# Attention issued from one written list of tasks, with a buffer for each pair's transposed V

## The chip, the cores and the metric

One Trainium2 chip, one core of it. The metric is device time in microseconds (us) of one execution; the median of several executions is compared. Five queues matter: PE (TensorE), DVE (VectorE), ACT (ScalarE), POOL (GpSimd) and SP (SyncE, which issues nearly all DMAs here). Each runs its instructions strictly in the order in which they stand in its program, and waits on semaphores of the others.

## What is computed

Sparse attention over 2 batches of 8 heads (768 positions of 64), then two MLP blocks. All in float32.

```python
def _attn_ref(q, k, v):                       # S = 768, block 32, window 16
    k_sum = k.reshape(B, H, nb, block, D).max(axis=3)
    v_sum = v.reshape(B, H, nb, block, D).mean(axis=3)
    scores_l = scale * q @ k.T                # kept where |i - j| < window
    scores_s = scale * q @ k_sum.T + log(block)
    a = softmax(concat([scores_l masked, scores_s]))
    return a @ concat([v, v_sum])
...
x = attn_out as (B, S, 512)
h = relu(x.T @ w_tok1) @ w_tok2;  u = x + h.T      # tokens, 256 wide
x = u + relu(u @ w_ch1) @ w_ch2                    # channels, 1536 wide
xn = (x - mean) / sqrt(var + 1e-6) * g_ln
out = x + relu(xn @ w2_ch1) @ w2_ch2               # channels, 2048 wide
```

## The kernel before

**Pairs and quads.** Two heads share the 128 partitions and make a *pair*; there are 8 pairs (0 to 3 are batch 0). A pair's 768 rows go in 12 windows of 64 rows, four of them a *quad*: quad n = 3i + qd belongs to pair i, n runs from 0 to 23. A window has 96 keys around it and 24 block keys, 120 columns (`NK`).

**One quad, step by step** (methods of `Kern`): `att_qk` puts the scores into one of two score banks (PE). `att_exp` does two things, for each of four windows: a DVE instruction adds the mask and takes the row's extreme (L453), an ACT instruction takes the exponential (L463). `att_tr` transposes the weights on PE (L470), `att_evac` copies them to SBUF on ACT (L477), `att_av` multiplies by V (PE, L489), `att_norm` divides and stores into `u` (DVE, L503, L506).

**One pair.** `load_pair` issues K and Q on SP; `prep_k` takes the block maximum of K on DVE (L338), `copy_k` writes it into the K tile on ACT (L348). For pairs 0 to 3 V comes transposed into `VT` (`load_vt`, L318): `prep_v1` sums blocks of 32 (for pair 0 one DVE reduce, L360; for pairs 1 to 3 a tree of ten POOL additions, L366 to L370), `prep_v2` writes the sums into `VT` (ACT, L386), `att_vtr` transposes four windows on PE (L409) and `att_vev` copies them into `V` (ACT L418 for the first quad of a pair, DVE L420 for the others). For pairs 4 to 7 V is loaded in its final form (`load_v`) and only its sums are made, from `vt`: a POOL tree (L377, L380), one transpose on PE (L395), ACT (L397), POOL copies (L401). K, Q and V have three buffers, `VT` two.

**Work of the next block inside attention.** `g1(b, hf)` is x.T @ w_tok1 in pieces of twelve PE passes (L518), `g2(b)` the second token product in pieces of six matmuls (L300 to L302), `transpose_u` the transposes of u (L561). `fill` issues matmuls on zeros whose result nobody reads (L1125). Beside it the first weights are loaded (`load_half`, tiles `stage`, three buffers) and converted: `words` on ACT (L131), `decode` on DVE (L149, L154), `split_hi` on ACT (L201), `split_lo` on DVE (L226). Halves 0 to 2 hold the token weights (`tok`).

**What sets the order.** `attention` gives each of these steps a number, quad index plus an offset from the table `ORDER`, sorts, and calls them in that order. Only PE is under `manual_schedule`: its instructions stand as called. DVE, ACT, POOL and SP are ordered by the framework's scheduler from its own estimates and from priorities. The first loads and twelve fills are called in `run`, ahead of `attention`.

```python
ORDER = {
    "load_k": -5.2, "load_vt": -5.1, "load_v": -4.7, "kmax": -1.3, "copy_k": -1.0, "vsum": -2.4,
    "vput": -0.2, "vsum0": 0.55, "vput0": 1.6, "exp": 0.5, "tr": 1.1, "evac": 1.55, "av": 2.15,
    "norm": 2.6, "vtr": 1.3, "vev": 1.4, "load_vk": -2.65, "lo": 2.7, "conv": 3.5, "bg": 8.58, "fin": 0.97,
}
```

After attention come the channel MLPs, here the *main part*; its first instruction on PE is the matmul of the tile g_('u', 0)_3.

Of the kernel before, what the change touches and what calls it, by code (L numbers as in the profile page):

```python
# [20 lines left out]
P = 128  # L21
# [30 lines left out]
NT = 4  # L52
SCALE = 1.0 / math.sqrt(D)
# [6 lines left out]
class Kern:  # L60
# [46 lines left out]
    def conv_tick(self):  # L107

        nc = self.nc
        n = self.tick  # L110
        self.tick += 1
        lag = self.lag
        if 0 <= n - lag + 1 < NHALF:
            self.split_hi(n - lag + 1)
        if self.wide:
            if n < NHALF:
                yield from self.words(n)
            if 0 <= n - 1 < NHALF:
# [22 lines left out]
    def decode(self, h):  # L141


        nc = self.nc
        t = self.raw.pop(h)
        m = self.dec[h].bitcast(U32)
        put = nc.vector.scalar_tensor_tensor
        if h < EARLY or h % 2:
            nc.vector.tensor_scalar(m, m, 3, None, op0=ALU.logical_shift_left)  # L149
            yield  # L150
            if h < EARLY:
                yield
                yield
            put(m, t[:, :, 0], 29, m, op0=ALU.logical_shift_right, op1=ALU.bitwise_or)  # L154
        else:
            put(m, t[:, :, 1], 3, m, op0=ALU.logical_shift_left, op1=ALU.bitwise_or)  # L156

    def conversion(self):

        while self.tick < NHALF + self.lag:  # L160
            h = self.tick - self.lag + 1
            if 1 <= h <= NHALF and h - 1 not in self.half:
# [19 lines left out]
    def load_half(self, h):  # L182
        if self.wide:
# [7 lines left out]
    def split_hi(self, h):  # L191
        x = self.dec[h] if self.wide else self.raw[h]
        if h < 3:
            if not self.wide:
                self.nc.scalar.copy(self.tok[:, h], x)
            return
# [116 lines left out]
    def flat_vt(self, i):  # L313
        return self.VT[i % 2].rearrange("p v c -> p (v c)")

    def load_vt(self, i):
        if i < NT:
            self.nc.sync.dma_start(self.VT[i % 2][:, 0:6, NB : NB + 160], self.vk[i])  # L318
        else:
            self.nc.sync.dma_start(self.flat_vt(i)[:, 0:S], self.vt[i - NT])  # L320
# [12 lines left out]
    def prep_k(self, i):  # L333
# [3 lines left out]
        with self.tc.issue_after(self.ttr[3 * i - 2].ins) if i > 0 else ExitStack():  # L337
            nc.vector.tensor_reduce(  # L338
                ks.rearrange("p (v j) -> p v j", v=6),
                K[:, 0:6, NB + 16 : NB + 144].rearrange("p v (j k) -> p v j k", k=BLOCK),  # L340
                axis=AX.X,
                op=ALU.max,
            )
        self.ks[i] = ks

# [6 lines left out]
    def prep_v1(self, i):  # L352
        nc = self.nc
        if i < NT:
            zs = self.att.tile([P, NB], F32, tag="vs", bufs=2, name=f"vs{i}")
            x = self.VT[i % 2][:, 0:6, NB + 16 : NB + 144].rearrange("p v (j k) -> p v j k", k=BLOCK)
            z = zs.rearrange("p (v j) -> p v j", v=6)
            if i == 0:
                with self.tc.issue_after(self.ttr[0].ins):
                    nc.vector.tensor_reduce(z, x, axis=AX.X, op=ALU.add)  # L360
            else:
                for v in (0, 3):
                    half = self.att.tile([P, NB // 2, BLOCK // 2], F32, tag="vh", bufs=1, name=f"vh{i}_{v}")
                    h = half.rearrange("p (v j) k -> p v j k", v=3)
                    n = BLOCK // 2
                    nc.gpsimd.tensor_tensor(h, x[:, v : v + 3, :, 0:n], x[:, v : v + 3, :, n : 2 * n], op=ALU.add)  # L366
                    while n > 2:
                        n //= 2
                        nc.gpsimd.tensor_tensor(half[:, :, 0:n], half[:, :, 0:n], half[:, :, n : 2 * n], op=ALU.add)
                    nc.gpsimd.tensor_tensor(zs[:, 4 * v : 4 * v + 12], half[:, :, 0], half[:, :, 1], op=ALU.add)  # L370
# [3 lines left out]
        cur = self.flat_vt(i)[:, 0:S].rearrange("p (n k) -> p n k", k=BLOCK)  # L374
# [7 lines left out]
    def prep_v2(self, i):  # L382
        nc = self.nc
        if i < NT:
            zs = self.vs.pop(i)
            nc.scalar.activation(  # L386
                self.VT[i % 2][:, :, 0:NB],
# [5 lines left out]
        V, Z = self.V[i % 3].rearrange("p (j w) c -> p j w c", j=2), self.Z[i % 2]  # L393
        ps = self.ps_pt.tile([P, 512], F32, tag="pt", name=f"psv{i}")
        nc.tensor.transpose(ps[:NK, 0:P], Z, self.ident)  # L395
        src = self.att.tile([NK, P], F32, tag="zs", bufs=1, name=f"zs{i}")
        nc.scalar.activation(src, ps[:NK, 0:P], AF.Copy, scale=1.0 / BLOCK)  # L397
# [14 lines left out]
    def att_vev(self, n):  # L412
        nc = self.nc
# [28 lines left out]
    def att_exp(self, n):  # L442
# [5 lines left out]
        pr = self.att.tile([P, 4, NK], F32, tag="pr", bufs=3, name=f"pr{n}")  # L448
        self.pr[n] = pr
        for u in range(4):  # L450
            w = 4 * qd + u
            mv = w % 2 if 0 < w < NW - 1 else 2 + w % 2
            self.ttr[n] = nc.vector.tensor_tensor_reduce(  # L453
# [9 lines left out]
            nc.scalar.activation(pr[:, u], sn[:, u], AF.Exp, bias=mn[:, u : u + 1], scale=-1.0)  # L463
# [49 lines left out]
    def g1(self, b, hf):  # L513
        nc = self.nc
        for t in range(2):
            ps = self.ps_mm.tile([P, 512], F32, tag="mm", name=f"g1_{b}_{hf}_{t}")
            for st in range(ST):
                nc.tensor.matmul(  # L518
                    ps[:, :256],
                    self.tok1(st, t),  # L520
                    self.u[:, b * ST + st, 256 * hf : 256 * hf + 256],
                    start=st == 0,
                    stop=st == ST - 1,
                )
            yield
            cs = slice(256 * hf, 256 * hf + 256)
            hh, hl = self.hh[b][:, t, cs], self.hl[b][:, t, cs]
            nc.scalar.activation(hh, ps[:, :256], AF.Relu)
            nc.vector.scalar_tensor_tensor(hl, ps[:, :256], 0.0, f32(hh), op0=ALU.max, op1=ALU.subtract)  # L529
            yield  # L530

    def g2(self, b):
        nc = self.nc
        for st in range(ST):
# [20 lines left out]
    def transpose_u(self, g):  # L555
        nc = self.nc
        th, tl = self.new_xt(("u", g))
        for cc in range(CC):
# [6 lines left out]
            nc.scalar.copy(th[:, cc], ps[:, :GN])  # L565
            nc.vector.tensor_tensor(tl[:, cc], ps[:, :GN], f32(th[:, cc]), op=ALU.subtract)
# [501 lines left out]
    def attention(self):  # L1068


        npair, nq = B * NPAIR, 3 * B * NPAIR
        O = ORDER
        ev = []
        put = lambda at, *fns: ev.append((at, len(ev), fns))
        for i in range(npair):
            at = 3 * i
            if i > 1:
                put(at + O["load_k"], lambda i=i: self.load_pair(i))
                put(at + O["load_vt" if i > NT + 1 else "load_vk"], lambda i=i: self.load_vt(i))
                put(at + O["load_v"], lambda i=i: self.load_v(i))  # L1080
            put(at + (O["kmax"] if i != 1 else -0.46), lambda i=i: self.prep_k(i))
            put(at + (O["copy_k"] if i != 1 else -0.44), lambda i=i: self.copy_k(i))
            put(at + O["vsum"] if i else O["vsum0"], lambda i=i: self.prep_v1(i))
            put(at + O["vput"] if i else O["vsum0"] + 0.01, lambda i=i: self.prep_v2(i))
        for n in range(nq):
            put(n, lambda n=n: self.att_qk(n))
            if n < O["bg"]:
                put(n + 0.02, lambda: self.fill(2))
                put(n + 0.25, lambda n=n: self.fill(1 if 2 < n + 1 < 3 * NT else 2))
            if n < 3 * NT:  # L1090
                put(n + O["vtr"], lambda n=n: self.att_vtr(n))
                put(n + O["vev"], lambda n=n: self.att_vev(n))
            put(n + O["exp"], lambda n=n: self.att_exp(n))
            put(n + O["tr"], lambda n=n: self.att_tr(n))
            put(n + O["evac"], lambda n=n: self.att_evac(n))
            put(n + O["av"], lambda n=n: self.att_av(n))
            put(n + O["norm"], lambda n=n: self.weave(self.att_norm(n), self.convert(self.ops)))
        put(0.0, lambda: self.load_half(0), lambda: self.load_half(1))
        put(O["conv"], lambda: setattr(self, "ops", 4))
        put(O["bg"], lambda: setattr(self, "ops", 2))  # L1100
# [319 lines left out]
```

## Time and profile before

| | |
|---|---|
| median of 3 executions | 594.06 us (592.63 to 597.55) |
| the profiled execution | 593.27 us, span of its trace 591.5 us, mean granted clock 0.986 |
| busy over the span | PE 567.7 us (96%), DVE 405.8, ACT 271.8, POOL 30.0 |
| moved by DMA | 135.76 MB |
| first score matmul | 6.38 us after the span's start |
| end of the score matmuls of quad 11 | 56.14 us |
| first matmul of the main part | 114.20 us |

Times of day in the trace count from the span's start. A busy time of PE is not PE at its peak: neighbouring matmuls overlap in the records, so the price of a piece is taken from its start to the next one's start. "Granted clock" is 1 at TensorE's upper level, 2.4 GHz, and a half at its lower, 1.2 GHz; a mean between says that a stretch had both.

### The profile page before, as it was taken

The numbers are of one execution on the slowest core, as the hardware profiler recorded it, in microseconds if no ns is written. First come the engines' busy times: TensorE is split into PE (matmuls) and PEld (weight loads), VectorE is DVE, ScalarE is ACT, GpSimd is POOL, SyncE is SP. The second block draws the span as 40 slices with busy tenths as digits, with TensorE's granted clock in tenths as the row PEclk, the third lists the DMA queues.
The fourth block names the chain that finished last, engine by engine and source line by source line (L and its number), as shares of the span: only waits on it lengthen the run. The fifth ranks groups of instructions, "written<-read, shape, count | busy, mean of one in ns | idle before, by whom it ended". The sixth has DMA issues, their size and how long they took to land.

```text
span 591.5 us, 10312 instructions
## 1 busy us (share of the span) xinstructions
PE 567.7 (96%) x3688; PEld 501.3 (85%) x3693; DVE 405.8 (69%) x980; ACT 271.8 (46%) x602; POOL 30.0 (5%) x71
## 2 busy tenths in 40 slices
PE   5788999999999999999999979999999999999997
PEld 2566777889898898999899868888889899999997
DVE  3687566464876788656648956586977687767781
ACT  2676545423874656535668513445423223223320
POOL 1142621000000000000000000000000000000000
PEclk9799999999999999999999989999999999999999
DMA  9798810043678887798947787587887998777645
GB/s 294 237 282 263 261 43 3 2 142 100 189 236 275 301 287 262 262 343 285 325 160 244 222 281 245 167 278 227 277 287 267 335 303 278 250 229 226 192 145 176
DMA packets 63656, 135.76 MB, mean 230 GB/s; under 512 B 5747, under 2 KB 22899, under 8 KB 63606
## 3 DMA queue, kind: packets, MB, share of 16 engines
q1 hardware_dynamic: 63600, 135.09, 69.4%
q8 instruction: 29, 0.48, 0.3%
q14 instruction: 21, 0.17, 0.1%
q10 hardware_dynamic: 6, 0.02, 0.0%
HBM read 100.49 MB, written 34.60 MB: 228 GB/s over the span
## 4 chain that ended last, share of the span: by engine, by line
PE 71%; DMA 14%; DVE 7%; POOL 3%; ACT 3%; issue 2%; SPq 0%; ACTq 0%; POOLq 0%
PE m L300 6%; PE m L302 6%; PE m L301 6%; DMA stage<-in_wts_dram 3%; DMA slot<-w2s 3%; DMA VT<-in_vk_dram 3%; PE acc_x L302 3%; PE acc_x L301 3%; PE acc_x L300 3%; PE g L518 2%; PE acc_y L302 2%; PE acc_y L301 2%; PE acc_y L300 2%; DMA w1s<-sps 2%; PE av L489 1%
## 5 line engine op out<-in xcount | busy, mean ns | idle before, releaser
L300 PE MATMUL m<-slot,slot 128*128 128x384 f32 (+1 forms) x141 | 48.0, 341 | 4.7 <-ACT sm L830 3.6
L302 PE MATMUL m<-slot,slot 128*128 128x384 f32 (+1 forms) x141 | 47.2, 335 | 0.0
L301 PE MATMUL m<-slot,slot 128*128 128x384 f32 (+1 forms) x141 | 47.2, 335 | 0.0
L302 PE MATMUL acc_x<-slot,al 128*128 128x512 f32 x96 | 38.1, 397 | 0.0
L301 PE MATMUL acc_x<-slot,ah 128*128 128x512 f32 x96 | 38.0, 396 | 0.0
L300 PE MATMUL acc_x<-slot,ah 128*128 128x512 f32 x96 | 37.9, 395 | 0.0
L463 ACT ACTIVATE pr<-sn,mn 128x120 f32<-128x120 f32 x96 | 30.3, 384 | 13.1 <-DVE mn L453 13.1
L300 PEld LDWEIGHTS m<-slot,slot 128*128 128x128 f32 x141 | 26.7, 189 | 8.3 <-ACT sm L830 4.3
L301 PEld LDWEIGHTS m<-slot,slot 128*128 128x128 f32 x141 | 26.8, 190 | 1.5
L809 ACT ACTIVATE ah<-sm 128x384 fp32r<-128x384 f32 x16 | 8.4, 525 | 40.9 <-DVE sm L818 40.9
L302 PEld LDWEIGHTS m<-slot,slot 128*128 128x128 f32 x141 | 26.8, 190 | 0.0
L154 DVE SCALAR_TENSOR_TENSOR dec<-stage,dec 128x512 uint32<-128x512 uint32 x36 | 24.8, 690 | 0.7
L131 ACT ACTIVATE dec<-stage 128x512 f32<-128x512 f32 x36 | 24.1, 673 | 1.8 <-DMA stage<-in_wts_dram 1.8
L453 DVE CUSTOM_DVE_ANT_0 sn<-scores,mask 128x120 f32<-128x120 f32 x96 | 21.3, 277 | 4.3 <-PE scores L433 4.2
L518 PE MATMUL g<-u,tok 128*128 128x256 f32 x96 | 22.5, 386 | 0.3 <-DVE hl L529 0.3
L302 PEld LDWEIGHTS acc_x<-slot,al 128*128 128x128 f32 x96 | 18.2, 189 | 4.0
L156 DVE SCALAR_TENSOR_TENSOR dec<-stage,dec 128x512 uint32<-128x512 uint32 x23 | 15.9, 691 | 7.3 <-ACT stage L131 7.3
L226 DVE TENSOR_TENSOR slot<-dec,slot 128x512 fp32r<-128x512 f32 x27 | 18.5, 687 | 2.8 <-ACT slot L201 2.8
L518 PEld LDWEIGHTS g<-u,tok 128*128 128x128 f32 x96 | 17.7, 190 | 3.2 <-DVE hl L529 0.5
L245 DVE TENSOR_TENSOR sp<-dec,sp 128x512 fp32r<-128x512 f32 x16 | 11.0, 685 | 13.7 <-ACT sp L211 13.7
L302 PE MATMUL acc_y<-slot,al_s 128*128 128x256 f32 x72 | 20.1, 280 | 0.0
L301 PE MATMUL acc_y<-slot,ah_s 128*128 128x256 f32 x72 | 20.1, 279 | 0.0
(1496 smaller groups left out, 1740.8 us busy)
## 6 DMA issues: line engine op xcount, KB each, us to landing
stage<-in_wts_dram SPq DMA_DIRECT2D x62, 512.0 KB, 4.7
slot<-w1s SPq DMA_DIRECT2D x94, 256.0 KB, 3.7
w1s<-sps SPq DMA_DIRECT2D x16, 512.0 KB, 4.1
w2s<-sp SPq DMA_DIRECT2D x16, 512.0 KB, 3.7
slot<-w2s SPq DMA_DIRECT2D x16, 512.0 KB, 4.8
w2t<-wk SPq DMA_DIRECT2D x16, 512.0 KB, 4.9
slot<-w2t SPq DMA_DIRECT2D x8, 768.0 KB, 5.2
slot<-w2s SPq DMA_DIRECT2D x22, 256.0 KB, 4.3
```

The costliest lines, as they stand in the source:

```text
L131: fold = lambda out: nc.scalar.activation(out, high, AF.Prelu, scale=2.0**-112, alpha=-(2.0**32))
L154: put(m, t[:, :, 0], 29, m, op0=ALU.logical_shift_right, op1=ALU.bitwise_or)
L156: put(m, t[:, :, 1], 3, m, op0=ALU.logical_shift_left, op1=ALU.bitwise_or)
L226: nc.vector.tensor_tensor(wl, x, f32(wh), op=ALU.subtract)
L245: nc.vector.tensor_tensor(buf[:, 512:1024], x, f32(buf[:, 0:512]), op=ALU.subtract)
L300: nc.tensor.matmul(out, lhs[0], rhs[0], start=first, stop=False)
L301: nc.tensor.matmul(out, lhs[0], rhs[1], start=False, stop=False)
L302: nc.tensor.matmul(out, lhs[1], rhs[0], start=False, stop=last)
L453: self.ttr[n] = nc.vector.tensor_tensor_reduce(sn[:, u], ps[:, u % 2, u // 2, :NK], self.mask[:, mv], scale=-SCALE, scalar=3e38, op0=ALU.a ...
L463: nc.scalar.activation(pr[:, u], sn[:, u], AF.Exp, bias=mn[:, u : u + 1], scale=-1.0)
L518: nc.tensor.matmul(ps[:, :256], self.tok1(st, t), self.u[:, b * ST + st, 256 * hf : 256 * hf + 256], start=st == 0, stop=st == ST - 1,)
L809: nc.scalar.activation(ah, x, AF.Relu)
```

## The change

`attention` no longer computes an order. A string `FRONT` of 389 tasks is read from left to right; a letter is the step and the number its quad, pair, weight half or piece. All of PE, DVE, ACT, SP and POOL stand in the order of this list. The opening loads and the fills are tasks of it too. `att_exp` is cut into its DVE half `m` and its ACT half `e`, `prep_v2` for the later pairs into three, and pieces of `g1`, `g2`, `transpose_u` can be called singly and in any order, with their evacuation as tasks of their own. For pairs 0 to 3 there is one transposed V tile each (`VW0` to `VW3`, the pool `wide`), whose space is given to `xtile` when they are done (`close_wide`, task `b`); `VT` shrinks to two plain tiles for pairs 4 to 7. The block sums of pairs 1 to 3 are one DVE reduce each, as pair 0's was. Of the twelve `att_vev` copies ten are on ACT (`x`) and two on DVE (`X`); before it was four and eight. There are 33 fills, before 41. Halves 0 to 9 of the weights are handled by tasks (`W`, `D`, `C`, `O`).

```diff
+FRONT = """
+l0 f f f f y1 f f y0 f f f v0 f f f l1 f f f f k0 f v1 f f y2 f f K0 l2 q0 f m0 f f v2 e0 f f h0 q1
+h1 t0 s0 v3 f c0 f f m1 f S0 e1 w0 k1 q2 x0 t1 m2 l3 K1 a0 e2 w1 h2 n0 q3 x1 s1 c1 t2 w2 c2 m3 a1 S1
...
+"""
...
     def load_vt(self, i):
         if i < NT:
-            self.nc.sync.dma_start(self.VT[i % 2][:, 0:6, NB : NB + 160], self.vk[i])
+            self.nc.sync.dma_start(self.wide[i][:, 0:6, NB : NB + 160], self.vk[i])
...
         if i < NT:
             zs = self.att.tile([P, NB], F32, tag="vs", bufs=2, name=f"vs{i}")
...
-            if i == 0:
-                with self.tc.issue_after(self.ttr[0].ins):
-                    nc.vector.tensor_reduce(z, x, axis=AX.X, op=ALU.add)
-            else:
-                for v in (0, 3):
-                    half = self.att.tile([P, NB // 2, BLOCK // 2], F32, tag="vh", bufs=1, name=f"vh{i}_{v}")
...
-                    nc.gpsimd.tensor_tensor(zs[:, 4 * v : 4 * v + 12], half[:, :, 0], half[:, :, 1], op=ALU.add)
+            nc.vector.tensor_reduce(z, x, axis=AX.X, op=ALU.add)
             self.vs[i] = zs
...
-    def att_vev(self, n):
+    def att_vev(self, n, copy):
...
-        if qd == 0:
-            nc.scalar.copy(out, src)
-        else:
-            nc.vector.tensor_copy(out, src)
+        copy(out, src)
...
-    def att_exp(self, n):
+    def att_min(self, n):
...
+    def att_exp(self, n):
+        sn, mn = self.sn.pop(n)
+        self.pr[n] = self.att.tile([P, 4, NK], F32, tag="pr", bufs=3, name=f"pr{n}")
...
+        do = {
+            "f": lambda _: self.fill(1),
+            "q": self.att_qk,
+            "m": self.att_min,
+            "e": self.att_exp,
+            "t": self.att_tr,
+            "c": self.att_evac,
+            "w": self.att_vtr,
+            "x": lambda n: self.att_vev(n, nc.scalar.copy),
+            "X": lambda n: self.att_vev(n, nc.vector.tensor_copy),
+            "a": self.att_av,
+            "n": lambda n: self.weave(self.att_norm(n)),
+            "k": self.prep_k,
+            "K": self.copy_k,
+            "s": self.prep_v1,
+            "S": self.prep_v2,
...
+            "l": self.load_pair,
+            "v": self.load_vt,
+            "r": self.load_v,
+            "h": self.load_half,
...
+            "W": self.tok_words,
+            "D": self.tok_decode,
+            "b": lambda _: self.close_wide(),
+            "C": self.split_hi,
+            "O": lambda h: [0 for _ in self.split_lo(h)],
+            "g": lambda k: next(piece[k]),
+            "G": lambda k: next(piece[k]),
+            "H": lambda k: next(piece[k]),
+        }
+        with tc.manual_schedule(engines={E.Activation, E.DVE, E.SP, E.Pool}):
+            for t in FRONT.split():
+                do[t[0]](int(t[1:] or 0))
```

`g` issues a piece on PE, `G` and `H` its evacuation; `k` and `K` are the two steps on K, `s` and `S` those on V's sums, `l`, `v`, `r`, `h` the loads. In the main part the calls are as they were, but for one row of seven counts of conversion steps in its first product (from 2 in each to 2, 2, 2, 2, 2, 1, 0).

At the opening of ACT, before (`K_135`, `VT_143`, `pr_216` and so on are the tiles K, VT, pr with a running number; VT_143 is pair 0's, VT_144 pair 1's):

```order
L348 COPY K_135<-ks_195 128x7x24 [waits DVE_49]
L463 ACTIVATE pr_216<-sn_214,mn_215 128x120 [waits DVE_49] x4
L386 ACTIVATE VT_144<-vs_228 128x7x24 [waits Pool_49]
L386 ACTIVATE VT_143<-vs_225 128x7x24 [waits DVE_49]
L131 ACTIVATE tok<-stage_206 128x512 [waits DMAHW4_49]
L463 ACTIVATE pr_268<-sn_266,mn_267 128x120 [waits DVE_49] x4
L477 COPY PT_138<-pt_253 120x512 [waits PE_49]
```

The same place with the change (VW_109 is pair 0's, VW_110 pair 1's):

```order
L369 COPY K_135<-ks_199 128x7x24 [waits DVE_49]
L477 ACTIVATE pr_229<-sn_220,mn_221 128x120 [waits DVE_49] x4
L493 COPY PT_138<-pt_248 120x512 [waits PE_49]
L395 ACTIVATE VW_109<-vs_253 128x7x24 [waits DVE_49]
L477 ACTIVATE pr_268<-sn_260,mn_261 128x120 [waits DVE_49] x4
L430 COPY V_140<-vtr_273 120x4x2x64 [waits PE_49]
L369 COPY K_136<-ks_278 128x7x24 [waits DVE_49]
...
L395 ACTIVATE VW_110<-vs_336 128x7x24 [waits DVE_49]
```

Pair 1's sums stood ahead of pair 0's and of the second exponential; now pair 0's stand alone there and pair 1's come seven instructions later.

On PE, around quads 9 to 11 (g is a piece of `g1`), before:

```order
L518 MATMUL g_0_0_0_671<-u,tok 128x256 x6
L433 MATMUL scores<-K_135,Q_132 64x120 x8
L470 MATMUL pt_698<-ident,pr_661 120x128 x4
L489 MATMUL av_703<-V_142,PT_139 64x65 x8
L409 MATMUL vtr_712<-ident,VT_143 120x128 x4
L518 MATMUL g_0_0_1_733<-u,tok 128x256 x6
L433 MATMUL scores<-K_135,Q_132 64x120 x8
```

The same place with the change:

```order
L443 MATMUL scores<-K_135,Q_132 64x120 x8
L423 MATMUL vtr_631<-ident,VW_112 120x128 x4
L505 MATMUL av_643<-V_142,PT_139 64x65 x8
L486 MATMUL pt_655<-ident,pr_602 120x128 x4
L443 MATMUL scores<-K_135,Q_132 64x120 x8
L533 MATMUL g_0_0_1_682<-u,tok 128x256 x6
L533 MATMUL g_0_0_0_713<-u,tok 128x256 x6
L486 MATMUL pt_729<-ident,pr_708 120x128 x4
```

Within a quad the order is now free from round to round, and the two pieces of `g1`, which stood a quad apart, stand together between quads 10 and 11.

On SP, the loads of pairs 3 and 4 before:

```order
L310 DMA K_135<-in_k_dram 128x6x160 [waits DMAHW1_49,DVE_49,PE_49]
L311 DMA Q_132<-in_q_dram 128x768 [waits DMAHW2_49]
L185 DMA stage_441<-in_wts_dram 128x1024 [waits DMAHW3_49,DMAHW4_49,DVE_49,Activation_49]
L185 DMA stage_495<-in_wts_dram 128x1024 [waits DMAHW5_49,DVE_49,Activation_49]
L318 DMA VT_143<-in_vk_dram 128x6x160 [waits PE_49]
L185 DMA stage_562<-in_wts_dram 128x1024 [waits DMAHW0_49,DMAHW6_49,DVE_49,Activation_49]
L310 DMA K_136<-in_k_dram 128x6x160 [waits DMAHW7_49,PE_49]
```

The same with the change:

```order
L340 DMA VW_112<-in_vk_dram 128x6x160 [waits DMAHW1_49]
L326 DMA K_135<-in_k_dram 128x6x160 [waits DMAHW2_49,DVE_49,PE_49]
L327 DMA Q_132<-in_q_dram 128x768 [waits DMAHW3_49]
L209 DMA stage_322<-in_wts_dram 128x1024 [waits DMAHW4_49]
L209 DMA stage_498<-in_wts_dram 128x1024 [waits DMAHW5_49,DMAHW7_49,DVE_49,Activation_49]
L342 DMA VT_143<-in_vt_dram 128x768 [waits DMAHW6_49]
L209 DMA stage_546<-in_wts_dram 128x1024 [waits DMAHW0_49,DVE_49,Activation_49]
L326 DMA K_136<-in_k_dram 128x6x160 [waits PE_49]
```

All four transposed V of batch 0 (VW) are issued ahead of pair 3's K, none of them waiting for PE; pair 4's K (K_136) still stands behind weight halves that wait for DVE and ACT.

## Rows read from the trace of the kernel before

**Rows 1.** Stretches of the span: busy time by engine, granted clock, DMA share, GB/s.

```profile
core 0: us, PE busy (x) PEld busy (x) DVE busy (x) ACT busy (x) POOL busy (x), PEclk, DMA share, GB/s
0.00:6.38 6.38, 5.19 (x13) 1.64 (x13) 2.25 (x5) 1.82 (x3) 0.67 (x9) 1.00 0.68 215
6.38:30.05 23.67, 15.81 (x191) 10.63 (x194) 12.87 (x57) 11.31 (x33) 3.39 (x10) 0.78 0.86 282
30.05:56.14 26.09, 22.64 (x279) 16.34 (x277) 21.43 (x84) 18.93 (x49) 9.29 (x21) 1.00 0.86 274
56.14:114.20 58.06, 56.21 (x637) 43.93 (x633) 35.04 (x162) 31.17 (x89) 16.62 (x32) 0.97 0.29 91
114.20:591.50 477.30, 467.82 (x2582) 428.78 (x2580) 334.24 (x673) 208.60 (x430) 0.00 (x0) 1.00 0.73 242
```

**Rows 2.** Timeline of PE in its opening: start, duration, instructions, idle time before.

```profile
1.19 5.26 PE L1125 MATMUL warm_ps<-warm 128*128 128x512 bf16 x12 [1.19 <-DVE warm L1192]
...
9.49 0.59 PE L1125 MATMUL warm_ps<-warm 128*128 128x512 bf16 x2
17.53 1.11 PE L409 MATMUL vtr<-ident,VT 128*120 128x128 f32 x4 [7.44 <-ACT VT L386]
```

**Rows 3.** Timeline of all engines around that wait.

```profile
8.64 0.95 DVE L360 TENSOR_REDUCE vs<-VT 128x24 f32<-128x768 f32 x1 [0.66 <-DMA VT<-in_vk_dram]
...
12.78 0.59 POOL L366 TENSOR_TENSOR vh<-VT 128x192 f32<-128x192 f32 x1 [11.57 <-DMA VT<-in_vk_dram]
...
16.90 0.57 ACT L386 ACTIVATE VT<-vs 128x168 f32<-128x168 f32 x2 [8.24 <-POOL vs L370]
```

**Rows 4.** Timeline of PE in a steady round, and at a piece of g1.

```profile
29.48 0.64 PE L433 MATMUL scores<-K,Q 64*64 64x120 f32 x16
30.05 0.61 PE L1125 MATMUL warm_ps<-warm 128*128 128x512 bf16 x2
30.49 0.60 PE L470 MATMUL pt<-ident,pr 128*120 128x128 f32 x4
31.02 0.69 PE L489 MATMUL av<-V,PT 121*64 121x65 f32 x16
31.64 0.39 PE L1125 MATMUL warm_ps<-warm 128*128 128x512 bf16 x1
...
43.64 2.76 PE L518 MATMUL g<-u,tok 128*128 128x256 f32 x12
46.33 0.64 PE L433 MATMUL scores<-K,Q 64*64 64x120 f32 x16
```

**Rows 5.** Timeline of DVE: its kinds of instruction.

```profile
27.60 0.27 DVE L453 CUSTOM_DVE_ANT_0 sn<-scores,mask 128x120 f32<-128x120 f32 x1
...
28.41 0.95 DVE L338 TENSOR_REDUCE ks<-K 128x24 f32<-128x768 f32 x1
29.27 0.17 DVE L503 RECIPROCAL rec<-av 128x4 f32<-128x4 f32 x1
29.48 0.42 DVE L506 TENSOR_TENSOR u<-av,rec 128x256 f32<-128x256 f32 x1
...
48.21 0.42 DVE L149 TENSOR_SCALAR dec<-dec 128x512 uint32<-128x512 uint32 x1
...
49.78 0.66 DVE L154 SCALAR_TENSOR_TENSOR dec<-stage,dec 128x512 uint32<-128x512 uint32 x1
```

**Rows 6.** Timeline of ACT: its kinds of instruction.

```profile
29.78 0.58 ACT L418 COPY V<-vtr 120x512 f32<-120x512 f32 x1
30.26 1.28 ACT L131 ACTIVATE dec<-stage 128x512 f32<-128x512 f32 x2
31.44 1.24 ACT L463 ACTIVATE pr<-sn,mn 128x120 f32<-128x120 f32 x4
```

**Rows 7.** Timeline of PE after a wait of a quad.

```profile
55.56 0.64 PE L433 MATMUL scores<-K,Q 64*64 64x120 f32 x16 [1.34 <-DVE mn L453]
...
57.65 1.11 PE L409 MATMUL vtr<-ident,VT 128*120 128x128 f32 x4
...
58.98 1.08 PE L433 MATMUL scores<-K,Q 64*64 64x120 f32 x16
...
61.60 0.65 PE L409 MATMUL vtr<-ident,VT 128*120 128x128 f32 x4
```

**Rows 8.** Waits of PE in the main part: us in total, times, longest.

```profile
PE m L300 <- ACT sm L830: 3.6, 1, 3.6
```

**Rows 9.** Waits of SP's queue up to 118 us: us in total, times, longest.

```profile
SPq L185 <- DVE dec L154: 51.9, 6, 41.3
SPq L310 <- PE scores L433: 8.8, 2, 8.3
```

More of the change, by code (lines that the diff above doesn't have):

```diff
@@ L154, in decode, with tok_words, tok_decode @@
             put(m, t[:, :, 0], 29, m, op0=ALU.logical_shift_right, op1=ALU.bitwise_or)
+            if h < 3:
+                self.half[h] = self.dec.pop(h)
         else:
             put(m, t[:, :, 1], 3, m, op0=ALU.logical_shift_left, op1=ALU.bitwise_or)
+    def tok_words(self, h):
+        for _ in self.words(h) if self.paired else ():
+            pass
+    def tok_decode(self, h):
+        if self.paired:
+            for _ in self.decode(h):
+                pass
+        else:
+            self.nc.scalar.copy(self.tok[:, h], self.raw.pop(h))
+            self.half[h] = self.tok[:, h]
     def conversion(self):
@@ L161, in conversion @@
             h = self.tick - self.lag + 1
[L162 removed]
+            if 4 <= h <= NHALF and h - 1 not in self.half:
                 for _ in self.split_lo(h - 1):
@@ L511, in att_norm, with g1, g2 @@
         )
-    def g1(self, b, hf):
+    def g1(self, b, hf, t):
         nc = self.nc
[L515 to L532, printed above, removed]
+        ps = self.ps_mm.tile([P, 512], F32, tag="mm", name=f"g1_{b}_{hf}_{t}")
+        for st in range(ST):
+            nc.tensor.matmul(
+                ps[:, :256],
+                self.tok1(st, t),
+                self.u[:, b * ST + st, 256 * hf : 256 * hf + 256],
+                start=st == 0,
+                stop=st == ST - 1,
+            )
+        yield
+        cs = slice(256 * hf, 256 * hf + 256)
+        hh, hl = self.hh[b][:, t, cs], self.hl[b][:, t, cs]
+        nc.scalar.activation(hh, ps[:, :256], AF.Relu)
+        yield
+        nc.vector.scalar_tensor_tensor(hl, ps[:, :256], 0.0, f32(hh), op0=ALU.max, op1=ALU.subtract)
+        yield
+    def g2(self, b, only=None):
         nc = self.nc
-        for st in range(ST):
+        for st in range(ST) if only is None else (only,):
             ps = self.ps_mm.tile([P, 512], F32, tag="mm", name=f"g2_{b}_{st}")
@@ L1085, in attention @@
[L1085 to L1097, printed above, removed]
@@ L1122, in fill @@
+        with self.tc.manual_schedule(engines={E.Activation, E.DVE, E.SP, E.Pool}):
+            for t in FRONT.split():
+                do[t[0]](int(t[1:] or 0))
     def fill(self, n):
@@ L1125, in fill @@
             self.nc.tensor.matmul(self.wps, self.warm[:, :P], self.warm, start=True, stop=True)
-    def begin(self, g):
-        if g in self.evacs:
-            self.end(g)
-        next(g)
-        self.evacs.append(g)
-    def end(self, g):
-        if g in self.evacs:
-            self.evacs.remove(g)
-            next(g)
-    def convert_until(self, halves):
-        while any(h not in self.half for h in range(halves)):
-            self.convert_all(1)
     def run(self):
```

177 lines of the change are left out of this document (70 added, 107 removed).

## The prediction

> **What bounds the kernel now.** I read the stretches of the span first. In the main part PE is busy 467.82 of 477.30 us at full clock [rows 1], and its longest wait there is 3.6 us [rows 8]. PE's order in the main part is the same in both programs, and it begins with the same weights loaded and converted (halves 0 to 8 decoded, 9 to 11 on their way). So the main part is taken as 477.30 us, whatever comes ahead, and the question is when it begins: at 114.20 us.
>
> The front has four stretches [rows 1]: 6.38 us to the first scores; 23.67 us to the end of quad 5's scores (30.05); 26.09 us to the end of quad 11's (56.14); 58.06 us to the main part. PE does the same useful pieces in each stretch under either list: the set of transposes, products and g1 pieces that stand ahead of quad 11's scores is the same (twelve scores, ten transposes of weights, ten of V, nine products with V, two pieces of g1). So the two fronts can be compared stretch by stretch.
>
> Next, what PE waits for. The largest hole is one row: PE stands still for 7.44 us, until 17.53, for ACT's L386 [rows 2]. The timeline of all engines shows why: pair 0's sums are made on DVE at 8.64 and take 0.95 us, but ACT starts its two L386 only at 16.90, released by POOL [rows 3]. The order on ACT explains it: pair 1's L386 stands ahead of pair 0's, and pair 1's sums are the POOL tree, which began at 12.78 when its load had landed. Behind the hole the granted clock of the stretch is 0.78 [rows 1] and the four transposes that end it take 1.11 us; the same four take 0.65 at 61.60 [rows 2, 7].
>
> In the third stretch no single wait is large. PE is recorded busy 22.64 of 26.09, fills among it, DVE 21.43 and ACT 18.93 [rows 1]: three engines near their limit pass work round. In the fourth PE is busy 56.21 of 58.06.
>
> **The prices.** From start to start, at full clock: scores of a quad 0.57 us, four transposes 0.53, products with V 0.62, a fill 0.22 (two from 30.05 to 30.49), a piece of g1 2.69 [rows 4]. DVE: a quad's four mask steps 0.81, a reduce over blocks 0.86, a division 0.55, a decode 0.42 and 0.66, taken as 1.0 together [rows 5]. ACT: a quad's exponentials 1.15, a copy out of PSUM 0.48, `words` 0.59 (half of the 1.18 from 30.26 to 31.44) [rows 6]. The small copies (K, sums, hh) I take at 0.25 us, an estimate from the 0.57 of two L386 [rows 3], and a split at 0.6, an estimate from the 0.66 of a DVE pass of the same size [rows 5].
>
> **First stretch, to the first scores.** The list puts 21 fills ahead of them, before it was 12. Twelve took 5.26 us, 0.44 each [rows 2], twice the later price, so they ran at the lower level although the column says 1.00. The scores at 6.38 followed at the higher level. Nine more at 0.22 add 2.0: start at 8.4 us. Ends: 6.4, if fewer are at the lower level; 10.4, if all 21 are (1.19 and 21 x 0.44). I take 8.4, a loss of 2.0.
>
> **Second, six quads.** Pair 0's sums now wait only for a DVE reduce that follows quad 0's mask steps, and pair 1's for one too. One reduce of 0.86 on DVE replaces ten POOL additions that took 4.1 us (from 12.78 to ACT's release at 16.90 [rows 3]); three pairs cost DVE 2.6 us, and six copies (each about 0.6, the DVE price of a pass of that size) go from DVE to ACT at 0.48. Work between the first scores and the end of quad 5's: PE 6 x 0.57 + 4 x 0.53 + 4 x 0.53 + 3 x 0.62 + 9 fills x 0.22 = 11.5 us; ACT 5 x 1.15 + 6 x 0.48 + 3 x 0.25 = 9.4; DVE 5 x 0.81 + 3 x 0.86 + 2 x 0.55 = 7.7. Lower end 11.5. Upper end: the old 23.67 without its hole, 16.2. The chain is short of slack only where V's sums, K of pair 1 and the first exponentials meet, so I take 13.3, nearer the lower end. Gain 23.67 - 13.3 = 10.4.
>
> **Third, quads 6 to 11.** Work by the list: PE 6 x 0.57 + 12 x 0.53 + 6 x 0.62 + 2 x 2.69 + 3 x 0.22 = 19.5 us; ACT 6 x 1.15 + 13 copies x 0.48 + 6 x 0.59 + 2 splits x 0.6 + 7 x 0.25 = 19.6; DVE 6 x 0.81 + 5 reduces x 0.86 + 5 x 0.55 + 5 x 1.0 + 2 x 0.6 + 2 x 0.4 = 18.9 (the 0.4 of an hl is L506's row, of the same size). Three engines at 19 to 20 us each, in fixed orders: lower end 19.6, upper end the old 26.1. Before, the scheduler put decodes and copies between a quad's mask steps by its own estimate; now they stand where the chain leaves room, but with equal loads somebody always waits. I take 22.5, the middle. Gain 3.6.
>
> **Fourth, to the main part.** The same pieces on PE. Before, 1.9 us were idle and the slow pieces around 57.65 to 61.60 cost half of their 4 us, 2.0. Lower end 54.2; four decodes and their splits that DVE had behind it before now fall in here (some 7 us on an engine busy 35 of 58 us), and three g1 pieces instead of two stand at the very end, which covers the last evacuations. Upper end 62, the old losses doubled. I take 58.0, no gain.
>
> **Sum.** 8.4 + 13.3 + 22.5 + 58.0 = 102.2 us to the main part, 12.0 earlier. The profiled execution took 593.27 (1.8 beside its span), so 581.3; the median of the runs is 0.8 above the profiled one: 582. Loads cost no extra bytes: the same tiles are read, in another order. The four larger V tiles cost space alone, and the tiles that inherit it are first written when the last V transpose lies several quads back; before, pair 2's V had to wait for pair 0's transposes, which now costs nothing.
>
> **Rival 1: denser still (571 to 578).** If the hand order reaches the row sums in the second and third stretch (11.5 and 19.6) and saves the slow pieces in the fourth, the main part begins some 5 to 10 us earlier again. For it: no engine is above 20 us of work in the third stretch. Against: all three are at 19 to 20.
>
> **Rival 2: the loads (586 to 592).** SP is strictly in order. A weight half waits for a free stage buffer, that is for a decode on DVE; before, SP waited 51.9 us for L154, though 41.3 of them at the end, where nothing hung on it [rows 9]. With the change pair 4's K stands behind halves 3 and 4, which wait for decodes 0 and 1, and pair 5's behind half 5. Up to pair 4's Q the list has moved 9.7 MB; from 6.38 us on, with 1.4 MB moved, at 282 GB/s [rows 1] that lands at 36 us, and DVE comes to its reduce about 38. If the decodes slip by some us, DVE stands at that reduce with a decode and quad 11's mask steps behind it, and everything moves by the slip. Price 4 to 10 us of the gain. Against: the landing is needed only after it, and by the end of quad 11 the list needs 10.2 MB (up to half 5, by the shapes of its tiles), where before 15.2 MB had moved by 56.14 (the three stretches' rates by their lengths).
>
> **Rival 3: slower, by the clock (599).** Of 41 fills 29 stood behind the first scores, the last at 43 us; now 12, the last one ahead of quad 7. A wait of 1.34 us ahead of the scores at 55.56 came just before pieces at half speed: the transposes at 57.65 took 1.11 us, the scores at 58.98 took 1.08 instead of 0.64 [rows 7]. If the third stretch ran wholly at the lower level, its PE work would be 39 us instead of 19.5, quad 11 would end at 8.4 + 13.3 + 39 = 60.7 instead of 56.14, and the time would be 593.27 + 4.6 + 0.8, 599. It decides from the point where the excess eats the 12 us: with 12 of 19.5 us of PE's work at the lower level. Against: the old third stretch kept 1.00 while PE rested 3.4 us of it, in short waits [rows 1], and useful work is now denser than it was with fills.
> The Trainium skill speaks for this rival, in "TensorE: Matmul & The Clock Gate", section "HAM oscillation — how this bites in real kernels": short bursts of matmuls with waits between them can put the array back to the lower clock at every burst. By that rule alone the sum would be the rival's 599; the trace agrees at 57.65 and speaks against it in the 26 us before.
>
> **Rival 4: the gain stays in the front (592 to 596).** The main part might start earlier and wait for weights. Against: PE waited in it 3.6 us at most at a time, and its conversion starts from the same state. Or the new order stalls as long elsewhere as the old one at 10 us.
>
> **How the numbers follow.** Forecast (578 to 586) 0.55; rival 1 0.20; rival 2 0.12; rival 4 0.07; rival 3 0.06. The time is the forecast's, 582. The range goes from 575 to 591: it holds the forecast, half of rival 1 and most of rival 2. About 1%, 6 us, is what a measurement of this kernel tells from no change. Faster by more: forecast, rival 1 and a third of rival 2, 0.79. Within: the rest of rival 2 and rival 4, 0.15. Slower: 0.06.
>
> **What would show it.** In the new profile: the first scores at 8.4 us; no wait of PE over 2 us between 9 and 25 us; the end of quad 5's scores near 22 and of quad 11's near 44 us; granted clock over 0.9 in that third stretch; the first matmul of the main part near 102 us and a main part of 477 us. I would be wrong if DVE waits for pair 4's K, if PE's pieces between 22 and 44 us take 1.1 us instead of 0.6, or if the main part is longer than it was.

## The result and the profile after

The changed kernel takes 569.64 us (568.82 to 570.52, 4 runs) against 593.35 before: ratio 0.959, 95% interval 0.954 to 0.965. That is twice the gain that was forecast. The profiled execution took 570.52, its span is 568.5.

The stretches of its span, cut at the same four marks (first scores, end of quad 5's, end of quad 11's, first matmul of the main part):

```profile
core 0: us, PE busy (x) PEld busy (x) DVE busy (x) ACT busy (x) POOL busy (x), PEclk, DMA share, GB/s
0.00:8.03 8.03, 6.84 (x21) 2.52 (x21) 2.25 (x5) 1.82 (x3) 0.68 (x9) 1.00 0.77 240
8.03:19.89 11.86, 11.80 (x186) 8.21 (x186) 9.27 (x50) 9.95 (x30) 0.00 (x0) 1.00 1.09 350
19.89:40.10 20.21, 19.87 (x272) 15.57 (x268) 19.07 (x79) 19.88 (x53) 2.67 (x6) 1.00 0.75 255
40.10:94.60 54.50, 52.42 (x637) 42.45 (x633) 40.10 (x172) 34.05 (x94) 15.31 (x26) 1.00 0.54 169
94.60:568.50 473.90, 466.32 (x2582) 427.33 (x2580) 334.04 (x673) 209.12 (x430) 0.00 (x0) 1.00 0.74 243
```

Against [rows 1], the first stretch is 1.6 us longer, the second 11.8 shorter, the third 5.9, the fourth 3.6, the main part 3.4: 23.0 of span. In the third, PE and ACT are recorded busy 19.9 of 20.2 us and DVE 19.1: three engines run at the same time with little left over. The clock column reads 1.00 throughout; in the first stretch it does so although the first fills take 0.43 us each there, twice as long as the later ones.

Timeline of PE in the opening, beside [rows 2]:

```profile
1.19 6.91 PE L1132 MATMUL warm_ps<-warm 128*128 128x512 bf16 x21 [1.19 <-DVE warm L1185]
8.03 0.64 PE L443 MATMUL scores<-K,Q 64*64 64x120 f32 x16
8.61 1.25 PE L1132 MATMUL warm_ps<-warm 128*128 128x512 bf16 x5
9.79 0.64 PE L443 MATMUL scores<-K,Q 64*64 64x120 f32 x16
...
11.93 0.65 PE L423 MATMUL vtr<-ident,VW 128*120 128x128 f32 x4
12.51 0.64 PE L443 MATMUL scores<-K,Q 64*64 64x120 f32 x16
```

Pair 0's V is transposed at 11.93 instead of 17.53, and no wait is printed. PE's longest waits in the whole execution (us in total, times, longest):

```profile
PE m L316 <- DVE um L836: 2.6, 4, 1.1
PE warm_ps L1132 <- DVE warm L1185: 1.2, 1, 1.2
PE scores L443 <- ACT pr L477: 1.0, 1, 1.0
PE psv L403 <- POOL Z L389: 1.0, 1, 1.0
```

Of the front three waits of 1 us or more are left (the last three rows), 1.2 us of them ahead of everything; and the 3.6 us of the main part [rows 8] are gone.

### The profile page after: what moved, and what is told of

Its sections match the earlier page's. It is cut to its first block, busy times and chain, and to the rows that moved or that the text cites. A ratio compares the mean times of both kernels' runs of the same rounds, so it can differ in the third digit from the quotient of the medians.

```text
span 568.5 us, 10249 instructions
## 1 busy us (share of the span) xinstructions
PE 557.3 (98%) x3685; PEld 496.1 (87%) x3685; DVE 404.7 (71%) x977; ACT 274.8 (48%) x608; POOL 18.7 (3%) x41
## 4 chain that ended last, share of the span: by engine, by line
PE 76%; DVE 7%; DMA 7%; ACT 6%; issue 2%; POOL 1%; ACTq 0%; POOLq 0%; DVEq 0%
PE m L316 7%; PE m L318 6%; PE m L317 6%; PE acc_x L318 3%; PE acc_x L317 3%; PE acc_x L316 3%; DMA slot<-w2s 2%; PE acc_y L318 2%; PE g L533 2%; PE acc_y L317 2%; PE acc_y L316 2%; ACT pr L477 2%; DMA w1s<-sps 1%; PE warm_ps L1132 1%; DMA stage<-in_wts_dram 1%
## 5 line engine op out<-in xcount | busy, mean ns | idle before, releaser
L141 ACT ACTIVATE dec<-stage 128x512 f32<-128x512 f32 x36 | 24.4, 677 | 2.4 <-DMA stage<-in_wts_dram 2.4
L533 PE MATMUL g<-u,tok 128*128 128x256 f32 x96 | 21.6, 381 | 0.0
L317 PE MATMUL acc_y<-slot,ah_s 128*128 128x256 f32 x72 | 20.1, 279 | 0.0
L623 ACT ACTIVATE xn<-u,nb,rs 128x128 f32<-128x128 f32 x48 | 20.1, 484 | 0.0
L316 PE MATMUL acc_y<-slot,ah_s 128*128 128x256 f32 x72 | 20.0, 278 | 0.0
```

The costliest lines, as they stand in the source:

```text
L141: fold = lambda out: nc.scalar.activation(out, high, AF.Prelu, scale=2.0**-112, alpha=-(2.0**32))
L316: nc.tensor.matmul(out, lhs[0], rhs[0], start=first, stop=False)
L317: nc.tensor.matmul(out, lhs[0], rhs[1], start=False, stop=False)
L533: nc.tensor.matmul(ps[:, :256], self.tok1(st, t), self.u[:, b * ST + st, 256 * hf : 256 * hf + 256], start=st == 0, stop=st == ST - 1,)
L623: nc.scalar.activation(xn[:, j], self.u[:, g * GT + j, cc * P : cc * P + P], AF.Identity, bias=nb[:, j : j + 1], scale=rs[:, j : j + 1],)
```

## The experiments

Times are medians; ratios are to the kernel before, run on the same chip, with a 95% interval in brackets. "Main part" is the span behind the last mark; stretches and main parts are those of one profiled execution of each kernel.

**The main part: the row of counts.** `c1_old_counts` gives the changed kernel the old row, `c2_new_counts` the kernel before the new one.

```diff
-self.convert_all(2 if n == 0 else (3, 2, 2, 3, 2, 0, 2)[k])
+self.convert_all(((2, 2, 2, 2, 2, 1, 0) if n == 0 else (3, 2, 2, 3, 2, 0, 2))[k])
```

> The changed kernel with the old row of conversion counts in the first product of the main part (2 in each of seven steps). Theory A (the 3.4 us by which the main part became shorter come from this row alone: with it the conversion step that waits for a spill buffer stands behind the copy that frees PE): the main part is 477 us again, the wait of PE for the copy L848 of 3.6 us is back, the time is 573, the ratio to before 0.966. Theory B (the main part is shorter because it begins from another state): 570, ratio 0.960, no such wait.

> The kernel before with the new row of counts in the first product, nothing else. Theory A: 590, ratio 0.994, and the wait of 3.6 us is gone. Theory B: 593.4, ratio 1.000, the wait stays.

Measured: c1 573.89 (0.969, 0.963 to 0.974), c2 588.06 (0.993, 0.990 to 0.996). c1's main part is 475.5 us, 1.6 more than with the new row where 3.4 were expected (its profiled execution took 571.96, 1.9 below the median), and has the wait again:

```profile
PE m L316 <- ACT sm L848: 3.1, 1, 3.1
```

c2's is 471.6 us and has it no longer. The row belongs to the first product of the second channel MLP, which in the trace before ends at about 347 us: it is not the first work of the main part in time, but it is the place of the wait of [rows 8]. The timeline of ACT there shows the cause. Before:

```profile
346.02 0.62 ACT L211 CAST sp<-dec 128x512 fp32r<-128x512 f32 x1 [7.67 <-DMA w1s<-sps]
346.55 0.52 ACT L809 ACTIVATE ah<-um 128x384 fp32r<-128x384 f32 x1
346.97 0.46 ACT L830 COPY sm<-m 128x384 f32<-128x384 f32 x1
```

With the old row put back (c1):

```profile
324.85 0.62 ACT L231 CAST sp<-dec 128x512 fp32r<-128x512 f32 x1 [7.22 <-DMA w1s<-sps]
```

With the change:

```profile
320.82 0.53 ACT L827 ACTIVATE ah<-um 128x384 fp32r<-128x384 f32 x1 [1.34 <-DVE um L836]
321.31 0.48 ACT L848 COPY sm<-m 128x384 f32<-128x384 f32 x1
326.86 0.62 ACT L231 CAST sp<-dec 128x512 fp32r<-128x512 f32 x1 [5.07 <-DMA w1s<-sps]
```

A cast that waits for a spill buffer's DMA stood ahead of the copy (`sm`) that PE needs; with three conversion steps fewer at the end of the product it stands behind. Before, the wait cost more than its 3.6 us: behind it, from 347.4 to 351.4 us, PE ran at a granted clock of 0.57. Theory A holds for the cause. Over all traces, the wait for `sm` stands in the four kernels with the old row (before, c1, d1 and h4, main parts of 475.5 to 478.4 us) and in none of the fourteen with the new one (471.1 to 475.7).

**Which engines' order.** The `with` over the list is narrowed:

```diff
-with self.tc.manual_schedule(engines={E.Activation, E.DVE, E.SP, E.Pool}):
+if True:                                                            # d2_scheduler
+with self.tc.manual_schedule(engines={E.Activation, E.DVE}):        # d3_act_dve
+with self.tc.manual_schedule(engines={E.SP, E.Pool}):               # d4_sp_pool
```

> The changed kernel with only PE in the order of the list; DVE, ACT, SP and POOL are ordered by the scheduler as before. Theory A (hand order on the other engines is what brings the third and fourth stretch to their sums of PE work): quads 6 to 11 in 23 to 26 us instead of 20.2, the time 575 to 583. Theory B (PE's order, the DVE sums and the four V tiles are enough): 570 to 572.

> The changed kernel with PE, ACT and DVE in the list's order and SP and POOL by the scheduler. If what the scheduler's kernel lost (578.4) lies in the order of ACT and DVE: 569 to 571. If it lies in the order of the loads: 576 to 579, with waits on DMA in the fourth stretch.

> The changed kernel with PE, SP and POOL in the list's order and ACT and DVE by the scheduler. If the loss lies in ACT and DVE: 576 to 579, second and third stretch 17 and 22 us as with all four by the scheduler. If in the loads: 569 to 571.

Measured: d2 578.44 (0.977, 0.971 to 0.983), d3 571.93 (0.966, 0.961 to 0.971), d4 579.48 (0.976, 0.972 to 0.981). Their main parts begin at 103.5, 96.8 and 103.8 us. d3 has the second and third stretch of the full list, 11.9 and 20.2 us; d2 has 17.5 and 21.8, d4 16.1 and 21.8. So it is ACT and DVE. What the order of SP and POOL adds (d3 against the full list, 0.966 and 0.959) is not told apart in time, since the two intervals overlap. Timeline of d4, all engines, where its second stretch loses most:

```profile
9.27 0.95 DVE L379 TENSOR_REDUCE vs<-VW 128x24 f32<-128x768 f32 x1 [3.77 <-DMA VW<-in_vk_dram]
...
10.65 0.95 DVE L360 TENSOR_REDUCE ks<-K 128x24 f32<-128x768 f32 x1 [0.43 <-DMA K<-in_k_dram]
11.52 0.27 DVE L462 CUSTOM_DVE_ANT_0 sn<-scores,mask 128x120 f32<-128x120 f32 x1
...
12.46 1.07 PE L443 MATMUL scores<-K,Q 64*64 64x120 f32 x16 [2.86 <-DVE mn L462]
```

The scheduler put pair 0's V sums and pair 1's K ahead of quad 0's mask steps on DVE; both wait for DMAs. Quad 0's scores had been there since 8.4 us, and quad 1's scores on PE wait for quad 0's mask steps. PE waits 2.86 us and comes back at half speed (1.07 for the same scores).

d3 has one long wait of PE left, in its fourth stretch (57.2 us against the list's 54.5). Timeline of ACT, DVE and PE there:

```profile
41.20 0.66 ACT L141 ACTIVATE dec<-stage 128x512 f32<-128x512 f32 x1 [2.71 <-DMA stage<-in_wts_dram]
41.89 0.43 DVE L159 TENSOR_SCALAR dec<-dec 128x512 uint32<-128x512 uint32 x1 [2.77 <-ACT dec L141]
43.91 0.64 PE L443 MATMUL scores<-K,Q 64*64 64x120 f32 x16 [2.75 <-DVE mn L462]
```

A weight half landed late, quad 11's mask steps stand behind its decode on DVE, and quad 12's scores wait for them. From 20 to 45 us d3 moved 8.07 MB, among them the V of later pairs, and a weight half took 8.8 us from issue to landing (median); in the list's kernel it was 6.15 MB and 3.7 us. So the order of the loads shows in the trace.

**The parts that are no order.** `d1_dve_sums`: before, with the POOL tree replaced. `h4_tiles_only`: before, with four tiles. `h1_parts`: both and the new counts, with `ORDER` and its scheduler. `h3_early_vt`: h1 with earlier offsets.

```diff
-            else:
-                for v in (0, 3):
...
+            else:                                                    # d1, h1, h3
+                with self.tc.issue_after(self.ttr[3 * i - 3].ins):
+                    nc.vector.tensor_reduce(z, x, axis=AX.X, op=ALU.add)
...
+        self.wide4 = [wide.tile([P, 7, 184], F32, name=f"VW{i}") for i in range(NT)]   # h1, h3, h4
+        put(12.5, self.close_wide)
...
-    "load_vt": -5.1, "load_vk": -2.65
+    "load_vt": -6.2, "load_vk": -6.2                                 # h3
```

> The kernel before with the block sums of pairs 1 to 3 as one DVE reduce each (the POOL tree removed), which also puts pair 0's sums ahead of pair 1's on ACT. Theory A (the hole at 10 us is the order on ACT; the rest of the front's gain is the hand order on all engines): hole under 2 us, first stretch of six quads 23.7 to about 15, third stretch as before at 25 to 27: 584 to 586, ratio 0.985 to 0.988. Theory B (most of the front's gain is this one edit): under 578, ratio under 0.975. Theory C (the hole is refilled by the next wait): 591 or more.

> The kernel before with the four transposed V tiles alone (POOL tree and old counts kept). On ACT pair 1's sums still stand ahead of pair 0's, so the hole of 7.4 us at 10 us stays. Theory A (the tiles matter by letting pair 2's and 3's V land early, after the hole): the third stretch gains 1 to 3 us: 590 to 592. Theory B (the tiles alone do what h1_parts had beyond sums and counts, 4 us): 588 to 590. Theory C (nothing without the sums): 593.5.

> The kernel before, its table ORDER and its scheduler kept, with the parts of the change that are no order: DVE block sums, four transposed V tiles whose space goes to xtile, the new row of counts. Theory A (the order is what counts, on PE by the list and on ACT and DVE by hand): no more than the two measured parts together, 2.9 for the sums and 5 for the counts: 585, ratio 0.987, quads 6 to 11 in 22 us and the stretch behind them in 60 us or more. Theory B (the parts suffice for what the list with the scheduler reached): 578 to 580.

> h1_parts (ORDER and scheduler as before, with DVE sums, four tiles and the new counts; 581.7) with only the transposed V loaded earlier: pairs 0 to 3 by 3.5 quads, pairs 4 to 7 by 1. Unlike in h2_parts_early_loads V itself keeps its offset, which there put its load ahead of the last use of the buffer, so that the last quad of a pair read the V of the pair three later and PE waited for it. Theory A (loads are no bound once the tiles are there): 580 to 583. Theory B (they are): 578 or less.

Measured: d1 590.29 (0.995, 0.992 to 0.999), h4 590.83 (0.994, 0.991 to 0.998), h1 581.73 (0.979, 0.973 to 0.985), h3 584.47 (0.983, 0.977 to 0.988). In d1 the hole at 10 us is gone (in its place PE waits 3.83 us at 15.1, for DVE's mask steps) and quad 11 ends at 49.1 instead of 56.1, but the main part begins at 113.0, only 1.2 us earlier (in a profiled execution of 593.21, 2.9 above the median). PE's timeline shows where it went:

```profile
56.94 0.64 PE L426 MATMUL scores<-K,Q 64*64 64x120 f32 x16 [0.55 <-DVE mn L446]
65.42 0.47 PE L388 MATMUL psv<-ident,Z 128*120 128x128 f32 x1 [4.00 <-POOL Z L373]
```

POOL in turn had waited for the transposed V of the second batch (idle 4.89 us until 59.47, released by VT's DMA). h4 keeps the hole, and its third stretch gains only 0.3 us of the 1 to 3 expected (25.8):

```profile
17.82 1.11 PE L415 MATMUL vtr<-ident,VW 128*120 128x128 f32 x4 [7.47 <-ACT VW L392]
```

h1 has neither; its wait is the next in line. On DVE pair 1's V sums, which wait for their load, stand ahead of quad 1's mask steps (the list has these sums behind quad 2's mask steps):

```profile
12.96 0.95 DVE L369 TENSOR_REDUCE vs<-VW 128x24 f32<-128x768 f32 x1 [3.02 <-DMA VW<-in_vk_dram]
...
14.77 1.08 PE L432 MATMUL scores<-K,Q 64*64 64x120 f32 x16 [3.75 <-DVE mn L452]
```

Sums (0.46%), tiles (0.56%) and counts (0.71%) add up to 1.7%; together they give 2.1% (1.5 to 2.7). Theory A of h1 was wrong in its number, 585, and in both its stretches: 25.1 and 57.0 us, where 22 and 60 or more were expected. The list with the scheduler (d2, 0.977) is not told apart from h1 (0.979): PE's own new order alone shows no gain. So of the 4.1% about half are these parts, and the rest comes with the order of the other engines (d2 to the list, 0.977 to 0.959); ACT's and DVE's alone bring 1.1 points of it (d3, 0.966). Loads brought forward (h3) gained nothing; in h3 those of pairs 4 and 5 also moved by 3.5 quads, not by 1.

`h2_parts_early_loads` also moved V's own load to -5.15. That puts it ahead of the last use of its buffer, so that a pair's last quad reads the V of the pair three later; PE waits for it, and its time tells nothing of the question.

> As the one before it, with the loads of V moved ahead in ORDER (transposed V of pairs 0 to 3 by 2.5 to 3.5 quads, that of pairs 4 to 7 by 1, V by half a quad). Theory A: what kept the sums' gain from arriving was V coming late behind quad 11; with the loads ahead the wait of PE for POOL's sums (4.0 us at 65 us in the kernel with DVE sums alone) goes: 580 to 583. Theory B (SP stands at weight halves whatever the offsets): as h1, within 2 us.

Measured: 595.83 (1.003). PE's timeline:

```profile
41.96 1.14 PE L488 MATMUL av<-V,PT 121*64 121x65 f32 x16 [8.17 <-DMA V<-in_v_dram]
```

**Single parts taken out of the list.** All five edit only `FRONT`, the sums or the tiles:

```diff
-... f v1 f f y2 f f K0 l2 q0            # e1_12_fills: the last nine f ahead of q0 go
-q0 f m0 f f v2 e0 f f ...               # e2_no_fills: every f behind q0 goes
-x1 x2 x4 x5 ...                         # f1_old_copies: X for every second and third quad of a pair
+X1 X2 X4 X5 ...
-nc.vector.tensor_reduce(z, x, ...)      # f2_pool_tree: pairs 1 to 3 by the POOL tree
-self.wide = [VW0, VW1, VW2, VW3]        # f3_two_tiles: two, v2 behind w2, v3 behind w5
+self.wide = [VW0, VW1, VW0, VW1]
```

> The changed kernel with 12 fills ahead of the first scores, as before, instead of 21. Theory A (the fills only delay; the clock needs no more than the old twelve): first scores at 6.4 us instead of 8.0, everything else keeps its length, the main part begins at 93, the time 568. Theory B (the nine extra fills keep the clock up through the thin first quads): pieces of the first six quads at 1.1 us instead of 0.6, the second stretch 13 us or more, no gain: 570 or more.

> The changed kernel without the 12 fills behind the first scores (21 ahead of them stay). Theory A (useful work is dense enough to hold the clock): granted clock stays 1.00 through the front, time 569 to 570.5. Theory B (rival 3, the clock): pieces at half speed somewhere between 9 and 25 us, the second stretch 14 to 18 us instead of 11.9, time 573 or more.

> The changed kernel with the V copies divided as before, four on ACT and eight on DVE, each where the list has it. Theory A (the third stretch holds because DVE and ACT are both just under PE): DVE gets six copies of 0.6 us more in the second and third stretch, which together grow by 2 to 4 us; 571.5 to 574. Theory B (the balance does not matter, since PE is the bound): 569 to 570.5.

> The changed kernel with pairs 1 to 3's block sums as the POOL tree again, each where the list has the DVE reduce. The tree takes 4.1 us from its load's landing, the reduce 0.9. Theory A (what cost time was where the sums' user stood on ACT, not the tree's length): the wait for them grows by about 3 us once, for pair 1, at 15 us, later ones are hidden; time 571 to 574. Theory B (the tree itself was the cost): second stretch back to 18 us or more, time 576 or more.

> The changed kernel with two transposed V tiles for pairs 0 to 3, as before, instead of four; pair 2's and pair 3's loads stand in the list right behind the last V transpose of pairs 0 and 1 (on SP they fall behind weight half 2 and pair 3's K, and wait for PE). Theory A (four tiles let SP run ahead; without them pair 2's V comes late once): V of pair 2 is issued at about 17 us instead of 10 and lands about 27 us, where its transposes stood at 24; third stretch 22 to 25 us instead of 20.2, time 572 to 576. Theory B (the tiles are not needed): 569 to 571.

Measured: e1 570.98 (0.963, 0.960 to 0.967), e2 572.16 (0.965, 0.962 to 0.969), f1 571.47 (0.965, 0.961 to 0.969), f2 570.16 (0.962, 0.959 to 0.965), f3 574.10 (0.969, 0.965 to 0.973); the list itself 0.959 (0.954 to 0.965). Only f3 lies well off, and its interval touches that of the list; the others are told apart by their traces alone.

e1: the first scores come at 6.42, and the main part begins at 94.9 all the same. The clock column stays at 1.00, as theory A has it, but the time is theory B's: of the 1.6 us 0.75 are left at quad 11 and none at the main part, lost to waits (0.57 us for mask steps at 9.0). e2: two waits early are followed by pieces at half speed, the main part begins at 97.2:

```profile
9.36 0.64 PE L431 MATMUL scores<-K,Q 64*64 64x120 f32 x16 [1.02 <-DVE mn L450]
...
11.50 0.82 PE L411 MATMUL vtr<-ident,VW 128*120 128x128 f32 x4 [0.92 <-ACT VW L383]
12.26 1.08 PE L431 MATMUL scores<-K,Q 64*64 64x120 f32 x16
13.27 1.11 PE L474 MATMUL pt<-ident,pr 128*120 128x128 f32 x4
14.30 1.11 PE L493 MATMUL av<-V,PT 121*64 121x65 f32 x16
15.35 0.65 PE L411 MATMUL vtr<-ident,VW 128*120 128x128 f32 x4
```

That is theory B's mechanism below its range: second stretch 13.3 us, not 14 to 18. f1: second and third stretch 12.3 and 21.6, 1.8 us more; main part from 95.9. f2: 12.7 and 20.2, the tree's length is hidden but for one wait of 0.65 us; main part from 96.1. f3: the third stretch grows to 24.4 around one wait,

```profile
25.68 0.69 PE L505 MATMUL av<-V,PT 121*64 121x65 f32 x16 [3.13 <-ACT V L430]
```

ahead of quad 6. It is the product of quad 4 (pair 1) that waits, for its V copy. Timeline of ACT:

```profile
24.80 0.34 ACT L395 ACTIVATE VW<-vs 128x168 f32<-128x168 f32 x1 [3.01 <-DVE vs L379]
25.05 0.57 ACT L430 COPY V<-vtr 120x512 f32<-120x512 f32 x1
```

The copy stands on ACT behind pair 2's sums, and pair 2's tile could only be loaded when pair 0's had been read.

**A further version.** `g1_swap` exchanges two pairs' loads and sums in the list:

```diff
-... v7 e17 h8 v6 ... s7 a15 H9 a16 ... s6 ...
+... v6 e17 h8 v7 ... s6 a15 H9 a16 ... s7 ...
```

> The changed kernel with the loads and the POOL sums of pairs 6 and 7 exchanged in the list, so that pair 6's, which PE transposes first (it waited 1.0 us for them at 72 us), come first. If PE's work sets the end of the front, that 1.0 us is gained: the main part begins at 93.6, the time 568.6. If the later sums of pair 7 wait in its place: 569.6, the same.

Measured: 568.56 (0.959, 0.956 to 0.962). Its main part begins at 93.35 with PE's wait at 72 us gone; in time it is the lowest median of all, but not told apart from the list.

## Why the prediction was wrong

The direction was right, and the hole at 10 us went for the reason given. The size was forecast at 12.0 us and measured at 23.7, and 569.64 lies below the range's 575 and even below rival 1's 571. By the prediction's own steps:

- *First stretch*, 8.4 us: measured 8.03. Right, and worth nothing: e1 shows that the 1.6 us do not reach the main part.
- *Second*, 13.3 (ends 11.5 and 16.2): 11.86. The step credited the reduce on DVE and ACT's order, but these are not enough: d1 and h1 lose the hole and keep 20.4 and 19.8 us. That the hole was ACT's order, as the step said, is shown by f2, which keeps the POOL tree and has no hole. The hand order of ACT and DVE made the rest (d3 11.9, d4 16.1); the waits that stay without it, in d1, h1 and d4, are for DVE.
- *Third*, 22.5 (19.6 and 26.1): 20.21. The failed step is its argument, "with equal loads somebody always waits". Under the list hardly anybody does (PE and ACT idle 0.3 us, DVE 1.1); under the scheduler, with the same work (d2, d4), the stretch takes 21.8, with `ORDER` as well 22.3 to 25.1 (d1, h1).
- *Fourth*, 58.0 (54.2 and 62): 54.50. It was taken as no gain, between its two ends. In the traces part of the gain goes with SP's order: d3, which has the list's ACT and DVE, has 57.2 us and the wait of 2.75 us for a late weight half. d2 has 56.5, d4 58.1.
- *Main part*, "taken as 477.30 us, whatever comes ahead": 473.90. The diff touches the counts of the very product whose 3.6 us wait was read off as the longest; the two were not joined. c1 and c2 show that they belong together: 0.7% of the time.

So three terms were put between their ends where the measured ones lie within 0.7 us of the lower end: 7.2 us too much in all; the main part 3.4; the first stretch 0.4. Together these are the 11.0 us between the span that was summed up (579.5) and the measured one. The time of 582 lies 12.4 above the measured median; most of the rest is that 0.8 us were added from the profiled execution to the median, while the measured median (569.64) lies 0.9 below the profiled execution (570.52). Rival 1, 571 to 578, came nearest and had a chance of 0.20.

Rival 2 did not come: DVE waits nowhere for pair 4's K. Rival 3's mechanism is real (e2) but small here: with the twelve fills kept behind the first scores, the clock column reads 1.00. The forecast's 582 is, by accident, what the parts without any list give (h1, 581.73).

What is open: how much of the last 2 us in time (d3 to the list) is SP's and POOL's order, since only the trace shows it; which of ACT's and DVE's orders gives how much, since they were only taken away together; and why loading earlier did not help h1.

## What to carry to other kernels

Here several in-order engines fed each other with equal work, and a good order came within 0.7 us of the sum of the fullest engine's prices; half-way to the old time is no neutral guess. An instruction that waits for a DMA, ahead in a queue of one whose operands are there, cost the consumer some 3 to 7 us here: look there first (pair 1's sums on ACT, V's sums on DVE, the cast for a spill buffer). A single hole filled gives little if the next late operand stands close behind it; and a one-line edit far from the change's centre is priced from the wait that stands at its line.

## What was not expected of the hardware

In the profiled executions of ten kernels with the same 21 fills ahead of them the first scores came at 7.30 to 8.44 us. The first fills start every 0.43 us and the later ones every 0.22, and the change falls at another moment in each (c1 has it earliest, f3 latest). The clock column reads 1.00 there all the time. In e2 two waits of 1.02 and 0.92 us were followed by 3 us at the lower level, 1.2 GHz (granted clock 0.52 from 12.2 to 15.4 us); in the list's kernel, with nine fills in these places, the granted clock reads 1.00 over the whole front.
